# A written order for the middle of a fused spectral-filter and MLP kernel

## The chip, the cores and the metric

The kernel runs on one core of one Trainium2 chip. The metric is the device time of one execution in microseconds (us). Times inside a kernel are those of its profiled execution, counted from its first instruction.

## The reference, cut to what matters

Two residual blocks follow each other: a 2-D Fourier filter over 2048 rows of 512 values, then a squared-ReLU MLP.

```
X = rfft2(layernorm(x));  X = X * (w_r + 1j * w_i);  h = x + irfft2(X, s=(S, D)).astype(bfloat16)
r = relu(layernorm(h) @ w1 + b1);  out = h + (r * r) @ w2 + b2          # S, D, F = 2048, 512, 1792
```

The kernel computes the Fourier transforms as matmuls with tables of sines and cosines.

## The kernel before

The stretch in question takes eight "pairs" of frequency rows, 0 to 7, from the second stage of the transform to the fourth. One pair goes through these steps:

- Stage 2 on TensorE, into PSUM. ScalarE copies the result to U.
- Stage 3 on TensorE. ScalarE copies the result to X if TensorE also did the butterfly (sum and difference of two halves), or else to AB, from which VectorE makes X by two instructions.
- VectorE: two products with W (mA, mB), two combinations (the two halves of Z) and, except for pairs 0, 5 and 6, two more (the halves of M).
- Stage 4 on TensorE, from M or, where there is none, from Z. ScalarE copies the result to T; for pair 7 VectorE copies one half of it.

After pair 7 come the last stages of the transform and then the MLP, in which TensorE is busy nearly to the end. The first of them, stage 5, multiplies T by the tables GIa and GIn. The prediction and the expectations call its start the start of the MLP. VectorE's part of a pair, before the change:

```python
    ON_PE = (2, 4, 6)                     # pairs whose butterflies TensorE does
    NO_M = (5, 6)
    def spectral(pr, between=None):
        X = Xs.pop(pr)
        nxt = butterfly(pr + 1) if pr + 1 < 8 and pr + 1 not in ON_PE else (lambda: None, lambda: None)
        # [cut: tiles mA, mB; the products X * W]
        if pr > 0:
            nxt[0]()
        nc.vector.tensor_tensor(Z[:, :, 0], mA[:, :, 0], mB[:, :, 1], ALU.subtract)
        nc.vector.tensor_tensor(Z[:, :, 1], mA[:, :, 1], mB[:, :, 0], ALU.add)
        # [cut]
        nxt[1]()
        if pr > 0 and pr not in NO_M:
            # [cut: tile M]
            nc.vector.tensor_tensor(M[:, 0], Z[:, 0], Z[:, 1], ALU.add)
            nc.vector.tensor_tensor(M[:, 1], Zf[:, 3::-3], Zf[:, 1:3], ALU.subtract)
```

So where no butterfly of the next pair lies between (pairs 0, 1, 3, 5 and 7), the first half of Z stands right behind the product that it reads, and the first of M right behind its Z. With two products that follow their butterfly directly (pairs 1 and 7), that makes ten such places. The fourth stage of a pair without M reads a table of negative cosines (`en`), which VectorE makes as Cn and a DMA transposes into EI.

```python
    def cos_negs():
        nc.vector.tensor_scalar(Cn[:], EF[:, 1, 1:8, :], -1.0, None, ALU.mult)
        turned(EI[:, 1:8, 3, :], Cn[:])                    # a transposing DMA on SyncE's queue
    # [cut] in stage4, for pairs 5 and 6:
            if M is None:
                en = ei[:, 2 * P:4 * P]
                mms = [(u, r, ei[:, P:3 * P]) for u in range(2)]
                mms += [(u, 1 - r, en if u == r else ei[:, 0:2 * P]) for u in range(2)]
    # [cut] ahead of the loop over the pairs:
    cos_negs()
    for k, (dst, src) in enumerate(((W1[:], ...), (W2[:], ...), (b1b[:], ...), (b2b[:], ...))):
        load = nc.sync.dma_start(dst, src)                 # the MLP's weights and biases, same queue
```

## Time and profile before

| kernel before | |
|---|---|
| time, median of 3 runs | 164.56 us (164.55 to 164.56) |
| span in the profile | 162.8 us |
| TensorE (PE) busy | 152.1 us, 93% |
| VectorE (DVE) busy | 125.4 us, 77% |
| ScalarE (ACT) busy | 105.5 us, 65% |
| pair 7's fourth stage starts on TensorE | 45.37 us |
| stage 5's first matmuls start | 46.88 us |

The shares average over stages with different limits. In the middle, from 22 to 46 us, TensorE, VectorE and ScalarE are all nearly full. The lines are shown in the prediction.

### The profile page before, as it was taken

The numbers are of one execution on the slowest core, as the hardware profiler recorded it, in microseconds if no ns is written. First come the engines' busy times: TensorE is split into PE (matmuls) and PEld (weight loads), VectorE is DVE, ScalarE is ACT, GpSimd is POOL, SyncE is SP. The second block draws the span as 40 slices with busy tenths as digits, with TensorE's granted clock in tenths as the row PEclk, the third lists the DMA queues.
The fourth block names the chain that finished last, engine by engine and source line by source line (L and its number), as shares of the span: only waits on it lengthen the run. The fifth ranks groups of instructions, "written<-read, shape, count | busy, mean of one in ns | idle before, by whom it ended". The sixth has DMA issues, their size and how long they took to land.

```text
span 162.8 us, 2720 instructions
## 1 busy us (share of the span) xinstructions
PE 152.1 (93%) x947; PEld 87.8 (54%) x947; DVE 125.4 (77%) x320; ACT 105.5 (65%) x203; POOL 36.9 (23%) x64
## 2 busy tenths in 40 slices
PE   3999899899987999999899999999999999999990
PEld 1367675677853874666345454434454444565470
DVE  6999899999957798699995588995379984377221
ACT  4989977999978780598552797731389760288000
POOL 7868850000000005025000235000052300052000
PEclk9999999999999999999999999999999999999999
DMA  5996299998000000200000100024300005210011
GB/s 128 361 277 123 62 201 185 366 367 183 11 0 0 4 0 2 66 5 0 0 32 33 36 0 0 2 64 101 92 4 2 0 0 129 64 36 0 3 62 34
DMA packets 16430, 12.34 MB, mean 76 GB/s; under 512 B 10784, under 2 KB 14880, under 8 KB 16416
## 3 DMA queue, kind: packets, MB, share of 16 engines
q1 hardware_dynamic: 16256, 11.25, 25.1%
q0 software_dynamic: 160, 0.92, 2.5%
q8 instruction: 7, 0.11, 0.3%
q14 instruction: 7, 0.06, 0.1%
HBM read 8.01 MB, written 2.10 MB: 62 GB/s over the span
## 4 chain that ended last, share of the span: by engine, by line
PE 66%; DVE 22%; ACT 4%; issue 3%; POOL 3%; ACTq 0%; DVEq 0%; POOLq 0%
PE po L726 26%; PE ph L693 25%; DVE act L697 3%; DVE st L217 3%; PE p L346 2%; DVE mA L436 2%; PE po L714 2%; DVE mB L436 2%; PE p L590 2%; DVE Z L442 1%; POOL rs L224 1%; DVE Z L443 1%; ACT rl L696 1%; PE p L563 1%; DVE M L452 1%
## 5 line engine op out<-in xcount | busy, mean ns | idle before, releaser
L696 ACT ACTIVATE rl<-ph,b1f 128x384 bf16<-128x384 f32 (+2 forms) x70 | 41.2, 615 | 22.5 <-PE ph L693 20.7
L693 PE MATMUL ph<-UT,W 128*128 128x384 bf16 (+2 forms) x280 | 51.6, 337 | 0.6 <-DVE UT L804 0.6
L726 PE MATMUL po<-W,act 128*128 128x512 bf16 x210 | 47.6, 379 | 0.0
L697 DVE TENSOR_TENSOR act<-rl 128x384 bf16<-128x384 bf16 (+2 forms) x70 | 31.3, 483 | 9.3 <-ACT rl L696 9.1
L700 POOL TENSOR_TENSOR hb<-hs,b2b 128x512 f32<-128x512 bf16 x16 | 18.6, 1166 | 87.0 <-DVE act L697 87.0
L693 PEld LDWEIGHTS <-W 128*128 128x128 bf16 x280 | 26.9, 98 | 21.2 <-issue 1.3
L726 PEld LDWEIGHTS <-act 128*128 128x128 bf16 x210 | 20.3, 98 | 24.8 <-issue 1.7
L730 DVE TENSOR_TENSOR ot<-po,hb 128x512 bf16<-128x512 f32 x15 | 10.3, 688 | 12.6 <-PE po L726 11.1
L257 PE MATMUL p<-ones 128*128 128x512 bf16 x23 | 8.2, 511 | 2.8 <-POOL ones L153 2.8
L594 DVE SCALAR_TENSOR_TENSOR hs<-p,xs 128x512 bf16<-128x512 f32 x14 | 9.1, 681 | 0.0
L243 PE MATMUL p<-KFr,xs 128*128 128x256 bf16 x32 | 7.7, 283 | 0.8 <-DVE KFr L228 0.8
L569 ACT CAST V<-p 128x512 bf16<-128x512 f32 x14 | 8.1, 593 | 0.0
L217 DVE BATCH_NORM_STATS2 st<-xs 128x6 f32<-128x512 bf16 x12 | 7.9, 677 | 0.0
L245 PE MATMUL p<-KFr,xs 128*128 128x256 bf16 x32 | 7.6, 281 | 0.0
L257 PEld LDWEIGHTS <-ones 128*128 128x128 bf16 x32 | 3.5, 115 | 6.7 <-POOL ones L153 2.8
L346 PE MATMUL p<-GF,Bt 128*128 128x256 bf16 x56 | 7.1, 273 | 0.0
L605 ACT ACTIVATE junk<-hs 128x512 bf16<-128x512 bf16 x6 | 3.8, 628 | 5.1 <-DVE hs L594 5.1
L491 ACT CAST T<-p 128x1024 bf16<-128x1024 f32 x7 | 7.1, 1041 | 0.0
L376 ACT CAST U<-p 128x1024 bf16<-128x1024 f32 x6 | 6.2, 1059 | 0.0
L346 PEld LDWEIGHTS <-Bt 128*128 128x128 bf16 x56 | 5.4, 98 | 1.3
L620 ACT ACTIVATE sd<-mv,eps 128x1 f32<-128x1 f32 (+2 forms) x10 | 2.7, 294 | 5.1 <-DVE mv L609 5.0
L582 DVE TENSOR_TENSOR H<-V 128x254 bf16<-128x254 bf16 x14 | 6.0, 426 | 0.0
(190 smaller groups left out, 228.7 us busy)
## 6 DMA issues: line engine op xcount, KB each, us to landing
W<-in_B_w_dram SPq DMA_DIRECT2D x2, 1792.0 KB, 10.6
out_dram<-ot SPq DMA_DIRECT2D x15, 128.0 KB, 1.8
xs<-in_A_x_dram SPq DMA_DIRECT2D x3, 512.0 KB, 6.7
WB<-in_A_w_r_dram SPq DMA_DIRECT2D x1, 578.2 KB, 6.4
WB<-in_A_w_i_dram SPq DMA_DIRECT2D x1, 578.2 KB, 7.6
xs<-in_A_x_dram SPq DMA_DIRECT2D x2, 256.0 KB, 3.4
b2b<-in_B_b_dram SPq DMA_DIRECT2D x1, 128.0 KB, 9.7
out_dram<-ot SPq DMA_DIRECT2D x2, 64.0 KB, 1.5
```

Of the source, the lines that this page charges most:

```text
L217: nc.vector.bn_stats(st[:], xs[:, g, :])
L243: nc.tensor.matmul(o, lhsT=xs[:, g, P * t:P * t + P], rhs=KFr[:, g, 0:P].unsqueeze(1).to_broadcast([P, 2, P]), start=True, stop=False)
L257: nc.tensor.matmul(o, lhsT=ones[:, 0:P], rhs=ones[:], start=True, stop=True)
L346: nc.tensor.matmul(puv[:, :, e, :], lhsT=Bt[:, 2 * t + 1 - e, 2 * pr + q, :], rhs=GFv[:, t, :, e, :], start=(t == 0), stop=(t == 1))
L569: nc.scalar.copy(V[:].rearrange("p e h c -> p (e h c)"), pe[:])
L594: nc.vector.scalar_tensor_tensor(hs[:, g, :], Ys.pop(g)[:], WSC, xs[:, g, :], ALU.mult, ALU.add)
L693: nc.tensor.matmul(ph[:, 0:n], lhsT=W1[:, d, bass.ts(f, P)], rhs=UT[:, d, 0:n], start=(d == 0), stop=(d == ND - 1))
L696: nc.scalar.activation(rl[:, 0:n], ph[:, 0:n], ACT.Relu, bias=b1f[:, f:f + 1], scale=1.0)
L697: sq = nc.vector.tensor_tensor(act[:, f, 0:n], rl[:, 0:n], rl[:, 0:n], ALU.mult)
L700: add = nc.gpsimd.tensor_tensor(hb[:, g, :], hs[:, g, :], b2b[:], ALU.add)
L726: nc.tensor.matmul(po[:], lhsT=act[:, f, bass.ts(i, P)], rhs=W2[:, f, :], start=(f == 0), stop=(f == NF - 1))
L730: nc.vector.tensor_tensor(ot[:], po[:], hb[:, g, :], ALU.add)
```

## The change

Its intent: replace the loops by one written list of steps, in which halves of Z and M of neighbouring pairs alternate, so that an instruction on VectorE rarely stands right behind the one that it reads from. Along with it, TensorE does the butterflies of other pairs, and the small sine table GIn is made first on ScalarE. The diff, cut to its core:

```diff
-    ON_PE = (2, 4, 6)
+    ON_PE = (4, 6, 7)
@@ spectral() is cut into single steps: butterfly(pr, h), times_w(pr, h), to_z(pr, h), to_m(pr, h)
+    def to_z(pr, h):
+        nc.vector.tensor_tensor(Zs[pr][:, :, h], mA[:, :, h], mB[:, :, 1 - h], ALU.add if h else ALU.subtract)
@@
-    cos_negs()
     for k, (dst, src) in enumerate(((W1[:], ...), (W2[:], ...), (b1b[:], ...), (b2b[:], ...))):
@@ the loop over the pairs goes; in its place:
+    ORDER = """
+        gn.0 s3.0 s3.1 s2.2 xa.0 cn.0 xb.0 x.1 u.2 s2.3 s3.2 s2.4 A.0 B.0 b.1 c.1 y.0 A.1 B.1 z.0 y.1 u.3 x.2
+        u.4 s3.3 s2.5 s4.0 s3.4 b.2 z.1 c.2 m.1 n.1 A.2 B.2 x.3 u.5 t.0 x.4 s4.1 s2.6 s3.5 b.3 y.2 c.3 z.2 A.3
+        B.3 m.2 n.2 A.4 y.3 B.4 z.3 y.4 m.3 z.4 t.1 u.6 gi.0 x.5 s4.2 s2.7 s3.6 b.5 m.4 n.4 c.5 n.3 A.5 B.5 u.7
+        t.2 x.6 s4.4 s3.7 s4.3 A.6 y.5 z.5 B.6 y.6 z.6 t.4 x.7 t.3 sq.0 s4.5 s4.6 A.7 B.7 y.7 z.7 m.7 n.7 t.5
+        t.6 s4.7 v.7 t.7
+    """
```

A step is a name and a pair. s2, s3 and s4 are stages on TensorE; u, x and t the copies by ScalarE (xa and v by VectorE); A and B the products; b and c the butterfly; y and z the halves of Z; m and n those of M. gn and gi make the sine tables GIn and GIa, sq readies the square root, and cn is the call of cos_negs, which thereby comes behind the four loads.

More of the change, by code (lines that the diff above doesn't have):

```diff
@@ L369, in stage2_one, with copy_by, u_copy @@
         cp(Us[pr][:, q].rearrange("p (r j e) -> p r j e", r=2, e=2), o.rearrange("p (r e j) -> p r j e", r=2, e=2))
+    P2, P3, P4, Ma = {}, {}, {}, {}
+    def copy_by(dve):
+        return nc.vector.tensor_copy if dve else nc.scalar.copy
     def stage2(pr):
-        new_u(pr)
-        pu = mm_tile("p2")
+        P2[pr] = pu = mm_tile("p2")
         for q in range(2):
             stage2_half(pr, q, pu[:, 512 * q:512 * q + 512])
-        nc.scalar.copy(Us[pr][:].rearrange("p q (r j e) -> p (q r) j e", r=2, e=2),
-                       pu[:].rearrange("p (q r e j) -> p (q r) j e", q=2, r=2, e=2))
+    def u_copy(pr, dve):
+        new_u(pr)
+        copy_by(dve)(Us[pr][:].rearrange("p q (r j e) -> p (q r) j e", r=2, e=2),
+                     P2.pop(pr)[:].rearrange("p (q r e j) -> p (q r) j e", q=2, r=2, e=2))
     def stage3(pr):
@@ L381, in stage3 @@
         if pr == 0:
-            Xs[pr] = X = fwd.tile([P, 2, 2, 256], BF16, tag="X", bufs=3, name="X")
-            pxs = [mm_tile("p3"), mm_tile("p3b")]
+            P3[pr] = pxs = [mm_tile("p3"), mm_tile("p3b")]
             for u, k1 in ((0, 0), (1, 8)):
@@ L389, in stage3 @@
                 nc.tensor.matmul(o[:, 256:512], lhsT=Sn, rhs=U[:, u, 0:256], start=False, stop=True)
-            for u, cp in ((0, nc.vector.tensor_copy), (1, nc.scalar.copy)):
-                cp(X[:, u].rearrange("p r c -> p (r c)"), pxs[u][:, 0:512])
         elif pr in ON_PE:
             C, Sp, Sn, Cm = EF[:, 1, pr, :], EF[:, 0, pr, :], EF[:, 2, pr, :], Cn[:, pr - 1, :]
-            px = mm_tile("p3")
+            P3[pr] = px = mm_tile("p3")
             for u in range(2):
@@ L404, in stage3 @@
                     nc.tensor.matmul(orr, lhsT=wc, rhs=U[:, 1, other], start=False, stop=(r == 1))
-            Xs[pr] = X = fwd.tile([P, 2, 2, 256], BF16, tag="X", bufs=3, name="X")
-            nc.scalar.copy(X[:].rearrange("p u r c -> p (u r c)"), px[:])
         else:
-            px = mm_tile("p3")
+            P3[pr] = px = mm_tile("p3")
             C, Sp, Sn = EF[:, 1, pr, :], EF[:, 0, pr, :], EF[:, 2, pr, :]
@@ L413, in stage3, with new_x, x_half, x_copy @@
             nc.tensor.matmul(px[:, 512:1024], lhsT=Sp, rhs=U[:, 0, :], start=False, stop=True)
+    def new_x(pr):
+        Xs[pr] = fwd.tile([P, 2, 2, 256], BF16, tag="X", bufs=3, name="X")
+    def x_half(pr, dve):
+        u = 0 if dve else 1
+        if u == 0:
+            new_x(0)
+        copy_by(dve)(Xs[0][:, u].rearrange("p r c -> p (r c)"), P3[0][u][:, 0:512])
+    def x_copy(pr, dve):
+        px = P3.pop(pr)[:].rearrange("p (u r c) -> p u r c", u=2, r=2)
+        if pr in ON_PE:
+            new_x(pr)
+            copy_by(dve)(Xs[pr][:], px)
+        else:
@@ L414, in stage3, with butterfly @@
             ABs[pr] = AB = fwd.tile([P, 2, 2, 256], BF16, tag="AB", bufs=3, name="AB")
             for u in ((0, 1) if pr == 1 else (slice(0, 2),)):
-                nc.scalar.copy(AB[:, u], px[:].rearrange("p (u r c) -> p u r c", u=2, r=2)[:, u])
-    def butterfly(pr):
+                copy_by(dve)(AB[:, u], px[:, u])
+    def butterfly(pr, h):
         AB = ABs[pr]
-        Xs[pr] = X = fwd.tile([P, 2, 2, 256], BF16, tag="X", bufs=3, name="X")
-        bsw = AB[:, 1, ::-1, :]
-        Xf = X[:].rearrange("p u r c -> p (u r) c")
-        return (lambda: nc.vector.tensor_tensor(Xf[:, 0::3], AB[:, 0], bsw, ALU.add),
-                lambda: nc.vector.tensor_tensor(Xf[:, 2:0:-1], AB[:, 0], bsw, ALU.subtract))
@@ L428, in spectral @@
-    def spectral(pr, between=None):
-        X = Xs.pop(pr)
-        nxt = butterfly(pr + 1) if pr + 1 < 8 and pr + 1 not in ON_PE else (lambda: None, lambda: None)
-        mA = fwd.tile([P, 2, 2, 256], BF16, tag="mA", bufs=2, name="mA")
-        mB = fwd.tile([P, 2, 2, 256], BF16, tag="mB", bufs=2, name="mB")
-        step = 16 - 2 * pr if pr else 8
-        for u in ((0, 1) if pr == 0 else (slice(0, 2),)):
-            for m, w in ((mA, WB[0]), (mB, WB[1])):
-                nc.vector.tensor_tensor(m[:, u], X[:, u], w[:, pr:pr + step + 1:step, 1:Df].unsqueeze(2)
-                                        .to_broadcast([P, 2, 2, 256])[:, u], ALU.mult)
-        Zs[pr] = Z = fwd.tile([P, 2, 2, 256], BF16, tag="Z", bufs=2, name="Z")
-        ABs.pop(pr, None)
-        if pr > 0:
-            nxt[0]()
-        nc.vector.tensor_tensor(Z[:, :, 0], mA[:, :, 0], mB[:, :, 1], ALU.subtract)
-        nc.vector.tensor_tensor(Z[:, :, 1], mA[:, :, 1], mB[:, :, 0], ALU.add)
-        if between:
-            between()
-        if pr == 0:
-            nxt[0]()
-        nxt[1]()
-        if pr > 0 and pr not in NO_M:
-            Ms[pr] = M = fwd.tile([P, 2, 2, 256], BF16, tag="M", bufs=2, name="M")
-            nc.vector.tensor_tensor(M[:, 0], Z[:, 0], Z[:, 1], ALU.add)
@@ new lines, in butterfly, with times_w @@
+        if h == 0:
+            new_x(pr)
+        Xf = Xs[pr][:].rearrange("p u r c -> p (u r) c")
+        nc.vector.tensor_tensor(Xf[:, 0::3] if h == 0 else Xf[:, 2:0:-1], AB[:, 0], AB[:, 1, ::-1, :],
+                                ALU.add if h == 0 else ALU.subtract)
+    def times_w(pr, h):
+        X = Xs[pr]
+        if h == 0:
+            Ma[pr] = [fwd.tile([P, 2, 2, 256], BF16, tag=t, bufs=2, name=t) for t in ("mA", "mB")]
+        step = 16 - 2 * pr if pr else 8
+        u = slice(h, h + 1) if pr == 0 else slice(0, 2)
+        for i in (range(2) if pr == 0 else (h,)):
+            nc.vector.tensor_tensor(Ma[pr][i][:, u], X[:, u], WB[i][:, pr:pr + step + 1:step, 1:Df].unsqueeze(2)
+                                    .to_broadcast([P, 2, 2, 256])[:, u], ALU.mult)
@@ L453, in spectral, with to_m @@
+    def to_z(pr, h):
+        mA, mB = Ma[pr]
+        if h == 0:
+            Zs[pr] = fwd.tile([P, 2, 2, 256], BF16, tag="Z", bufs=2, name="Z")
+        nc.vector.tensor_tensor(Zs[pr][:, :, h], mA[:, :, h], mB[:, :, 1 - h], ALU.add if h else ALU.subtract)
+    def to_m(pr, h):
+        Z = Zs[pr]
+        if h == 0:
+            Ms[pr] = fwd.tile([P, 2, 2, 256], BF16, tag="M", bufs=2, name="M")
+            nc.vector.tensor_tensor(Ms[pr][:, 0], Z[:, 0], Z[:, 1], ALU.add)
+        else:
             Zf = Z[:].rearrange("p u r c -> p (u r) c")
-            nc.vector.tensor_tensor(M[:, 1], Zf[:, 3::-3], Zf[:, 1:3], ALU.subtract)
+            nc.vector.tensor_tensor(Ms[pr][:, 1], Zf[:, 3::-3], Zf[:, 1:3], ALU.subtract)
@@ L456, in stage4 @@
     def stage4(pr, split=False):
         Z, M = Zs.pop(pr), Ms.pop(pr, None)
-        pts = [mm_tile("p4a"), mm_tile("p4b")] if split else [mm_tile("p4")] * 2
+        P4[pr] = pts = [mm_tile("p4a"), mm_tile("p4b")] if split else [mm_tile("p4")] * 2
         ei = EI[:, pr].rearrange("p k b -> p (k b)")
@@ L484, in stage4, with t_copy @@
                 nc.tensor.matmul(o, lhsT=M[:, 1, r, e::2], rhs=ei[:, 0:2 * P], start=False, stop=True)
-        dst = T2[:, :, :, 2 * pr:2 * pr + 2, :]
-        src = [pt[:].rearrange("p (l q g s) -> p l g q s", l=4, q=2, g=G) for pt in pts]
-        if split:
-            nc.scalar.copy(dst[:, 0:2], src[0][:, 0:2])
-            nc.vector.tensor_copy(dst[:, 2:4], src[1][:, 2:4])
-        else:
-            nc.scalar.copy(dst, src[0])
+    def t_copy(pr, dve):
+        sl = slice(0, 4) if pr < 7 else slice(2, 4) if dve else slice(0, 2)
+        copy_by(dve)(T2[:, sl, :, 2 * pr:2 * pr + 2, :],
+                     P4[pr][1 if pr == 7 and dve else 0][:].rearrange("p (l q g s) -> p l g q s", l=4, q=2, g=G)[:, sl])
     new_u(0)
@@ L506, with angle_tables @@
                 after(load, ga, "the rows of W first")
-    stage3(0)
-    stage3(1)
-    stage2(2)
-    for pr in range(9):
-        if pr == 1:
-            stage3(3)
-        if pr == 3:
-            stage3(5)
-        if pr + 3 < 8:
-            stage2(pr + 3)
-        if pr == 0:
-            stage3(2)
-        if pr == 0:
+    def angle_tables(k):
+        if k == 0:
             sin_of(GIa[:], fiI[:])
-        if pr == 2:
+        else:
             nc.scalar.activation(GIn[:], fiI[:, 0:1024].bitcast(I16)[:, ::2].rearrange("p (t c) -> p t c", t=4)[:, 0::2, :],
@@ L523, with to_sqrt @@
                                  ACT.Sin, scale=-SIN_SCALE)
-        if pr in (2, 4):
-            stage3(pr + 2)
-        if pr == 4:
-            stage3(7)
-        if pr > 0:
-            stage4(pr - 1, split=(pr == 8))
-        if pr == 8:
-            warm(mm_tile("idle")[:, 0:512], 2)
-        if pr == 0:
-            spectral(0)
-        elif pr < 8:
-            spectral(pr)
-        if pr == 5:
-            nc.gpsimd.tensor_copy(b1f[:], b1b[:])
-            nc.scalar.activation(junk1[:], eps[:], ACT.Sqrt, bias=eps[:])
+    def to_sqrt():
+        nc.gpsimd.tensor_copy(b1f[:], b1b[:])
+        nc.scalar.activation(junk1[:], eps[:], ACT.Sqrt, bias=eps[:])
@@ new lines @@
+    PIECES = dict(s2=stage2, u=u_copy, s3=stage3, xa=x_half, xb=x_half, x=x_copy, b=lambda k: butterfly(k, 0),
+                  c=lambda k: butterfly(k, 1), A=lambda k: times_w(k, 0), B=lambda k: times_w(k, 1),
+                  y=lambda k: to_z(k, 0), z=lambda k: to_z(k, 1), m=lambda k: to_m(k, 0), n=lambda k: to_m(k, 1),
+                  s4=lambda k: stage4(k, split=(k == 7)), t=t_copy, v=t_copy, gi=lambda k: angle_tables(0),
+                  gn=lambda k: angle_tables(1), sq=lambda k: to_sqrt(), cn=lambda k: cos_negs())
@@ new lines @@
+    ORDER = """
[5 more added lines that the diff above has]
+    """
+    for step in ORDER.split():
+        name, k = step.split(".")
+        if name in ("u", "x", "t", "xa", "xb", "v"):
+            PIECES[name](int(k[0]), k[1:] == "v" or name in ("xa", "v"))
+        else:
+            PIECES[name](int(k))
@@ L540 @@
+    warm(mm_tile("idle")[:, 0:512], 2)
     tab.release()
```

## The prediction

> **What bounds the kernel now.** I read the page first (spans and the share of each engine), then the chain of waits in order of time, then the timelines of VectorE, ScalarE and TensorE over the stage that the change rewrites, and last the issues of the DMA queue, because the list of the changed kernel shows that one transfer changes its place there.
>
> The change touches only the stretch from 21 to 47 us: pairs 0 to 7 go from the second DFT stage to the fourth. Three engines are nearly full there. These are the busy times from the first product with W to the last combination M, and of two parts of that stretch (columns: the stretch, its length, then PE, PEld, DVE, ACT, POOL, clock, DMA share, GB/s):
>
> ```profile
> 22.70:45.60 22.90, 21.66 (x179) 16.62 (x178) 22.24 (x52) 21.34 (x25) 0.40 (x1) 1.00 0.78 213
> 28.00:38.00 10.00, 9.53 (x85) 7.43 (x83) 9.69 (x24) 10.00 (x12) 0.00 (x0) 1.00 1.00 349
> 38.00:42.60 4.60, 4.60 (x39) 3.61 (x38) 4.57 (x11) 4.36 (x5) 0.29 (x1) 1.00 0.54 67
> ```
>
> No engine has more than 1.6 us of slack in 22.9. Which one ends last is told by the chain (start, length, what):
>
> ```profile
> 40.71 0.61 DVE mB L436
> ...
> 44.09 0.42 DVE Z L442
> 44.52 0.35 DVE Z L443
> 44.89 0.43 DVE M L452
> 45.37 0.40 PE p4a L464 x2
> ```
>
> From 30 to 45 us the chain is VectorE, one instruction after another; then it passes to the eight matmuls of pair 7, to the copies of T and to the MLP, where TensorE sets the time to the end. So a microsecond won or lost where pair 7's matmuls start (45.37) reaches the end whole.
>
> Within VectorE's row what can be won is small. Its timeline (start, length) shows it at pair 3:
>
> ```profile
> 32.53 0.69 DVE L436 TENSOR_TENSOR mB<-X,WB 128x1024 bf16<-128x1024 bf16 x1
> 33.25 0.42 DVE L442 TENSOR_TENSOR Z<-mA,mB 128x512 bf16<-128x512 bf16 x1
> 33.59 0.42 DVE L443 TENSOR_TENSOR Z<-mA,mB 128x512 bf16<-128x512 bf16 x1
> 34.12 0.43 DVE L452 TENSOR_TENSOR M<-Z 128x512 bf16<-128x512 bf16 x1
> 34.46 0.42 DVE L454 TENSOR_TENSOR M<-Z 128x512 bf16<-128x512 bf16 x1
> 34.79 0.69 DVE L436 TENSOR_TENSOR mA<-X,WB 128x1024 bf16<-128x1024 bf16 x1
> ```
>
> Independent neighbours start before the record of the earlier one ends: 0.34 us after a 512-wide one (34.12 to 34.46, length 0.43), 0.61 after a 1024-wide one. An instruction that reads what its neighbour wrote waits for the whole record plus 0.03: Z starts 0.72 after mB, M starts 0.53 after Z. Such a hold costs 0.11 us, at this M 0.19.
>
> The DMA queue (start, time in the issuing sequencer):
>
> ```profile
> 25.28 1.25 SPq L260 DMA_TRANSPOSE EI<-Cn  x1
> 26.64 1.10 SPq L503 DMA_DIRECT2D W<-in_B_w_dram  x2
> 27.79 4.95 SPq L503 DMA_DIRECT2D b1b<-in_B_b_dram  x1
> 32.78 5.71 SPq L503 DMA_DIRECT2D b2b<-in_B_b_dram  x1
> ```
>
> and from issue to landing:
>
> ```profile
> W<-in_B_w_dram SPq DMA_DIRECT2D x2, 1792.0 KB, 10.6
> ...
> b2b<-in_B_b_dram SPq DMA_DIRECT2D x1, 128.0 KB, 9.7
> ...
> EI<-Cn SPq DMA_TRANSPOSE x1, 3.1
> b1b<-in_B_b_dram SPq DMA_DIRECT2D x1, 3.5 KB, 14.5
> ```
>
> The turned negative cosines (EI from Cn) land at 25.28 + 3.1 = 28.4, before 3.7 MB of weights. The engines are then full to 38 (share 1.00 in the second row above), and the two biases land at 42.3 and 42.5 (27.79 + 14.5, 32.78 + 9.7).
>
> **What the Trainium skill says.** "VectorE: DVE Perf Modes", section "The DRAIN you can't avoid", has it that a semaphore between two operations costs nothing, and adds "A next op that is not held starts earlier". The trace agrees with the second sentence only: a dependent neighbour pays 0.11 us here. "DMA: Bandwidth & Descriptors", section "Queues, rings and completion order": one issuing engine owns one ring on each of the 16 engines, and descriptors of a ring are consumed in order. The trace agrees: W's first packets move just as the last of the transposes' do, at 27.7. "Perfetto Trace Analysis", section "DMA Instruction — HWDGE (DVE, Sync)": the recorded length of an issue is descriptor generation; the data move later. The trace agrees (a 4.95 us issue of 3.5 KB lands 9.5 us after its end). "ScalarE: Activation LUTs", section "What ACT_TABLE_LOAD costs", gives about 1283 ns; the trace has 1.28 us, and the change leaves it in place.
>
> **The change part by part.**
>
> 1. Which pairs have butterflies on TensorE: 2, 4, 6 become 4, 6, 7. Three before, three after: 12 matmuls against 4 each, and VectorE keeps 8 butterfly instructions (pairs 1, 2, 3, 5 instead of 1, 3, 5, 7). The counts of all work are the same: VectorE still has 14 products of 0.61, 4 of 0.34, 16 Z, 10 M and 8 X of 0.34: 8.5 + 1.4 + 11.4 = 21.3 us. Net 0.
>
> 2. The order on VectorE. Before, the first product starts at 22.70 and the last M is done with its slot at 45.57: 22.87 us, so 1.6 us are not work. I count ten holds by a neighbour (about 1.2 us) and 0.25 us at 29.66 to 29.91 for ScalarE's copy of AB. In the written order only three neighbours remain dependent: B.6 to y.6, B.7 to y.7, z.7 to m.7: 0.36 us. The first product starts about where it did (X's copy first, then Cn: 22.74). VectorE alone would be done at 22.74 + 21.3 + 0.36 = 44.4, 1.2 earlier. I laid the whole order out with these starts (matmuls every 0.109 us for 256 columns and 0.217 for 512; ScalarE's copies every 0.90), each instruction behind its producers and buffers. The same layout of the old order ends 0.4 us early, so I use differences only: pair 7's matmuls start 0.87 us earlier than in the old layout. TensorE (pair 6's stage 4 ends 43.9) and ScalarE (last T copy back to back) are then within 0.2 us of binding too, which is why it is 0.9 and not 1.2.
>
> 3. GIn first, GIa after u.6: the 0.5 us table fits before X's second copy, where ScalarE waited 0.28 us; the 1.1 us table no longer stands ahead of pair 3's AB. It is what removes the 0.25 us above; counted already.
>
> 4. A part that the words do not name: the instruction that makes the negative cosines, with its transpose, now stands behind the loads of W1, W2, b1 and b2 in the queue. Before it was ahead. Pairs 5 and 6 are the ones without M, and their fourth stage reads this table. All four loads move up by one transpose: W1 is issued at about 25.3 (its condition, the gathers, is met near 25.1) instead of 26.64, and its data gain about 1.05 us. b2b's issue ends at 38.49 - 1.3 = 37.2, the transpose is issued then, and in ring order its packets come behind b2b's. The last packets of b2b move at 41.8 before, so 40.7 now; 896 rows of 256 bytes took about 1.1 us before; the count lands 0.3 us later. That makes 42.1 us, an estimate.
>
> 5. In the layout pair 5's fourth stage begins at 40.5 (40.9 with the drift). Two matmuls need no new table, then TensorE, in order, stands until 42.1. Behind it are 30 matmuls of 0.109 (pairs 5 and 6) = 3.3 us, then pair 7: 45.4, against 45.37 before. ScalarE's copies of pairs 5, 6 and 7 follow the matmuls as before, so nothing more is added.
>
> The sum: VectorE's order -0.9, the late table +0.9, net about 0. After the middle nothing changes.
>
> **Rivals.** (a) The table does not bind. Speaking for it: transposes without a queue ahead take 2.4 to 3.1 us to land, which from 37.2 is 40.3, and the engines are only 0.54 busy from 38 to 42.6. Then the gain is 0.9: 163.65 us. (b) The table is later than I think, since its issue may have to wait for room as b2b's 5.71 us issue seems to have done, and one ring is slow (15 of b1's 16 counts land by 41.0, the last at 42.3). A landing at 43.5 costs 1.4: 166.0. (c) ScalarE becomes the bound: it is full for ten microseconds in the second row above. The layout has it idle 0.3 and 0.7 us early on and full at the end; a slip of 0.3 would leave a gain of 0.6 if (a) holds and nothing if the table binds. (d) TensorE: the 8 further matmuls of a pair on TensorE now come late (pair 7 instead of 2) and take 0.87 us near 38 to 40, but they are in the layout and cost nothing while the table is awaited.
>
> **Range and chances.** I give (a) or near it 0.3, the table near 42.1 with 164.2 to 165.0 0.45, and (b) 0.25. The middle is 164.5 us, the range 163.6 (no wait at all) to 165.8 (landing near 43.3). 2% is 3.3 us, far outside both: faster 0.01, same 0.98, slower 0.01.
>
> **What would show it.** VectorE's holds should shrink to three and its work up to z.6 end near 41.5. TensorE should stand for 1 to 2 us before the third matmul of pair 5's fourth stage, released by a DMA (EI from Cn) and not by VectorE; the last W landing should be about 1 us earlier; pair 7's matmuls should start near 45.4. I am wrong in step 4 if that transpose lands before 41 or after 43.3, and in step 2 if VectorE stands for other waits (a copy of AB or X by ScalarE, or a Z or M buffer still read by TensorE) for more than 0.3 us in all.

## The result, and the profile after

The changed kernel took 164.37 us (median of 4 runs: 164.48, 164.49, 164.15, 164.26). The kernel before in the same rounds took 164.56. The ratio is 0.9987, with a 95% interval of 0.9970 to 1.0004: the same. Ratios here are the mean time of one kernel's runs over that of the other's of the same rounds, so not quite the ratio of the medians quoted. Executions over 1.5% slower than the fastest of the same kernel are left out of the means.

The profile explains the first of those runs (164.48). The table arrived late, as foreseen. The chain of waits of the changed kernel (start, length, what):

```profile
37.48 4.24 DMA EI<-Cn
41.72 0.04 issue
41.77 3.45 PE p L500 x30
45.22 0.02 issue
45.24 0.70 ACT T L508
...
46.17 0.58 ACT T L508
46.75 0.05 issue
46.79 0.61 PE p L770 x4
```

Before, this stretch of the chain was VectorE. Now it is a DMA from 37.48 to 41.72, then 30 matmuls of pairs 5 and 6, then ScalarE's copies to T. Stage 5 starts at 46.79, against 46.88 before.

SyncE's queue shows why the transfer starts so late (start, time in the issuing sequencer):

```profile
25.48 0.94 SPq L520 DMA_DIRECT2D W<-in_B_w_dram  x2
26.47 5.03 SPq L520 DMA_DIRECT2D b1b<-in_B_b_dram  x1
31.55 5.83 SPq L520 DMA_DIRECT2D b2b<-in_B_b_dram  x1
37.48 2.20 SPq L260 DMA_TRANSPOSE EI<-Cn  x1
```

The same transpose was issued at 25.28 before. Now it stands behind the two issues of the biases, which hold SyncE for 10.9 us (how much of this is the biases' own doing is seen in e8).

TensorE's timeline (start, length, instruction, and in brackets the idle time before it with its releaser):

```profile
40.65 0.38 PE L500 MATMUL p<-EI,Z 128*128 128x256 bf16 x2
41.77 3.44 PE L500 MATMUL p<-EI,Z 128*128 128x256 bf16 x30 [0.73 <-DMA EI<-Cn]
45.04 0.38 PE L483 MATMUL p4a<-EI,M 128*128 128x256 bf16 x2
```

Two matmuls of pair 5's fourth stage run, the third waits 0.73 us for the table, and pair 7 starts at 45.04, 0.33 us earlier than before. Of this only 0.09 reaches stage 5, because of ScalarE. Its timeline in the changed kernel, and then the one line of the kernel before that answers to the last:

```profile
43.76 0.99 ACT L508 CAST T<-p 128x1024 bf16<-128x1024 f32 x1
45.24 1.01 ACT L508 CAST T<-p 128x1024 bf16<-128x1024 f32 x1 [0.48 <-PE p L500]
46.15 0.59 ACT L508 CAST T<-p4a 128x512 bf16<-128x512 f32 x1
```

```profile
46.24 0.58 ACT L488 CAST T<-p4a 128x512 bf16<-128x512 f32 x1 [0.19 <-PE p4a L464]
```

Before, ScalarE waited 0.19 us for pair 7's matmuls. Now it waits for nothing there: it begins pair 6's copy at 45.24, when TensorE has finished that pair, and is busy with it until 46.15.

VectorE did what the new order was written for. In this timeline of the changed kernel at pairs 3 and 4, halves of Z and M of different pairs stand side by side:

```profile
33.19 0.70 DVE L456 TENSOR_TENSOR mA<-X,WB 128x1024 bf16<-128x1024 bf16 x1
33.79 0.42 DVE L463 TENSOR_TENSOR Z<-mA,mB 128x512 bf16<-128x512 bf16 x1
34.13 0.70 DVE L456 TENSOR_TENSOR mB<-X,WB 128x1024 bf16<-128x1024 bf16 x1
34.73 0.76 DVE L463 TENSOR_TENSOR Z<-mA,mB 128x512 bf16<-128x512 bf16 x2
35.41 0.43 DVE L470 TENSOR_TENSOR M<-Z 128x512 bf16<-128x512 bf16 x1
```

Every start is 0.60 us after a product or 0.34 after a half; nothing is held. And the work up to z.6 is done near 41.7. Part of that lead is lost again: with TensorE standing, the buffer that the next Z needs is not free.

```profile
43.49 0.76 DVE L463 TENSOR_TENSOR Z<-mA,mB 128x512 bf16<-128x512 bf16 x2 [0.53 <-PE p L500]
```

This wait of 0.53 us is new (about 0.1 of it is the hold by B.7, the neighbour that Z reads), and is itself a consequence of the late table.

### The profile page after: what moved, and what is told of

It is laid out like the page before. It is cut to its first block, busy times and chain, and to the rows that moved or that the text cites. A ratio compares the mean times of both kernels' runs of the same rounds, so it can differ in the third digit from the quotient of the medians.

```text
span 162.7 us, 2708 instructions
## 1 busy us (share of the span) xinstructions
PE 149.7 (92%) x934; PEld 87.5 (54%) x947; DVE 124.8 (77%) x320; ACT 105.5 (65%) x203; POOL 36.7 (23%) x64
## 4 chain that ended last, share of the span: by engine, by line
PE 62%; DVE 22%; ACT 5%; issue 3%; DMA 3%; POOL 3%; ACTq 0%; DVEq 0%; POOLq 0%
PE po L742 26%; PE ph L709 21%; DVE act L713 4%; DVE st L217 3%; DMA EI<-Cn 3%; PE p L500 2%; PE po L730 2%; ACT rl L712 2%; PE p L346 2%; PE p L606 1%; POOL rs L224 1%; DVE Z L463 1%; DVE mB L456 1%; DVE mA L456 1%; DVE hs L610 1%
## 5 line engine op out<-in xcount | busy, mean ns | idle before, releaser
L742 PE MATMUL po<-W,act 128*128 128x512 bf16 x204 | 46.8, 379 | 0.3
L257 PE MATMUL p<-ones 128*128 128x512 bf16 x22 | 7.1, 461 | 2.9 <-POOL ones L153 2.8
L243 PE MATMUL p<-KFr,xs 128*128 128x256 bf16 x32 | 7.3, 272 | 2.2 <-DVE KFr L228 2.2
L245 PE MATMUL p<-KFr,xs 128*128 128x256 bf16 x32 | 7.3, 272 | 0.0
L463 DVE TENSOR_TENSOR Z<-mA,mB 128x512 bf16<-128x512 bf16 x16 | 6.3, 422 | 0.6 <-PE p L500 0.5
```

The source lines that it names most:

```text
L257: nc.tensor.matmul(o, lhsT=ones[:, 0:P], rhs=ones[:], start=True, stop=True)
L463: nc.vector.tensor_tensor(Zs[pr][:, :, h], mA[:, :, h], mB[:, :, 1 - h], ALU.add if h else ALU.subtract)
L742: nc.tensor.matmul(po[:], lhsT=act[:, f, bass.ts(i, P)], rhs=W2[:, f, :], start=(f == 0), stop=(f == NF - 1))
```

## The experiments

The theory T: the new order is worth most of a microsecond, and the late table, which came along with it, takes most of it back. The main rivals: A, ScalarE sets the end of the middle, whatever the table does; B, the order itself is worth little. Every kernel below gave correct results. The kernel before took 164.57 us in their rounds, without one slow run of 167.95 us, and 164.52 in those of e9, which ran on another chip than e1 to e8. The changed kernel was timed in rounds of its own, in which the kernel before took 164.56.

### e1: the table ahead of the loads again

The four loads are emitted behind the step cn.0. The order of the compute engines stays as written.

```diff
-    for k, (dst, src) in enumerate((...)):   # the four loads
-        load = nc.sync.dma_start(dst, src)
+    def weights():                           # the same loop, called later
-  cn=lambda k: cos_negs()
+  cn=lambda k: (cos_negs(), weights())
```

> The changed kernel with only the order in the DMA queue changed: the four weight and bias loads are issued behind the turned negative cosines instead of ahead of them; every engine's order stays. Theory T (the new VectorE order is worth 0.9 us and the late table gives most of it back): the table lands near 28.4 us, no wait for it, pair 7's matmuls start near 44.5 (45.04 in the changed kernel), total 163.6 to 163.8 us. Rival A (ScalarE's copies of T hold the end of the middle anyway): pair 7's matmuls come earlier, but the last T copies do not; total 164.1 to 164.4. Rival B (loads 1.3 us later matter for the MLP): total 164.4 or more.

Measured: 163.89 us (163.87 to 163.92), ratio 0.9958 (0.9944 to 0.9971). TensorE no longer waits for a DMA (its timeline):

```profile
40.66 3.66 PE L500 MATMUL p<-EI,Z 128*128 128x256 bf16 x32
44.36 0.39 PE L483 MATMUL p4a<-EI,M 128*128 128x256 bf16 x2
```

Pair 7 starts at 44.36, 1.01 us earlier than before. But the time fell by 0.68 only. ScalarE's timeline shows where the rest went:

```profile
40.33 1.01 ACT L432 CAST X<-p 128x1024 bf16<-128x1024 f32 x1 [0.58 <-ACT T L508]
41.24 1.02 ACT L508 CAST T<-p 128x1024 bf16<-128x1024 f32 x1
42.28 1.28 ACT L534 ACT_TABLE_LOAD   x1
43.57 0.30 ACT L534 ACTIVATE junk<-eps 128x1 f32<-128x1 f32 x1
43.77 1.90 ACT L508 CAST T<-p 128x1024 bf16<-128x1024 f32 x2
45.57 0.60 ACT L508 CAST T<-p4a 128x512 bf16<-128x512 f32 x1
```

From 40.33 to the last copy nothing waits. That copy starts 0.67 us earlier than before (46.24), not 1.01. The time lies between the two forecasts, 0.09 above T's range and 0.21 below A's. So T holds in the main: the changed kernel with the table early wins 0.68 us (its choice of pairs included, see e3), and the late table costs 164.37 - 163.89 = 0.48, give or take the spread of the changed kernel's runs (164.15 to 164.49). And A is partly right: ScalarE swallows 0.34 of what TensorE wins.

### e2: the late table in the old order

```diff
-    cos_negs()
     for k, (dst, src) in enumerate((...)):   # the four loads
         [cut]
+    cos_negs()
```

> The kernel before with only the negative cosines' transpose moved behind the four loads. Theory T: the table lands near 41.7 as in the changed kernel, but in the old order pair 5's fourth stage asks for it at 41.5, and TensorE has 0.43 us to spare before pair 7; so 0 to 0.15 us slower, 164.55 to 164.7. If a late table costs by itself what it took from the changed kernel (0.7 us), 165.2.

Measured: 164.57 us (164.55 to 164.81), ratio 1.0003 (0.9990 to 1.0017). The transpose landed at 41.70, as late as in the changed kernel. TensorE's timeline:

```profile
41.31 3.87 PE L481 MATMUL p<-EI,Z 128*128 128x256 bf16 x32
45.39 0.39 PE L464 MATMUL p4a<-EI,M 128*128 128x256 bf16 x2 [0.21 <-DVE M L452]
```

In the old order pair 5 begins 0.66 us later, so the table is hardly missed: the 32 matmuls take 3.87 us where they take 3.66 without a wait. TensorE has that time to spare, because it must wait for VectorE's first M of pair 7 in any case: 0.43 us in the kernel before, 0.21 here. So the late table costs something only where the order is fast enough to need it.

### e3: the choice of pairs alone

```diff
-    ON_PE = (2, 4, 6)      # in the kernel before
+    ON_PE = (4, 6, 7)
```

> The kernel before with only the choice of pairs changed: butterflies on TensorE for 4, 6, 7 in place of 2, 4, 6. Theory T: same counts, about one or two holds fewer on VectorE and pair 7's further matmuls on TensorE near 39 us, so 164.3 to 164.6 (-0.1 by the layout). A rival in which the choice of pairs, not the order, makes the gain on VectorE: 163.7 to 163.9.

Measured: 164.49 us (164.46 to 164.51), ratio 0.9994 (0.9981 to 1.0007). Pair 7 starts at 45.29 instead of 45.37. The choice of pairs is worth 0.08 us in the old order, no more.

### e4: the table later still

A load of 448 KB that nothing needs stands between W2 and the biases, ahead of the transpose.

```diff
                                     (W2[:], B_w2.rearrange("(i p) d -> p i d", p=P)),
+                                    (extra[:], B_w1[0:P]),
```

> The changed kernel with one further load of 448 KB between W2 and the biases (to a tile that nobody reads), so that the table comes later still. Theory T: at 365 GB/s it takes 1.25 us; the table lands near 43.0 and every bit of that reaches the end: total 165.5 to 165.8. Rival A (ScalarE holds the end): less than half of it, 164.4 to 165.0.

Measured: 168.12 us (166.83 to 168.69), ratio 1.0213 (1.0182 to 1.0245), which leaves it unclear whether it is 2% slower. I expected too small a delay: the profiled run is the fastest of them (166.83), and in it the transpose landed at 44.08, 2.36 us later than in the changed kernel. Its TensorE timeline:

```profile
44.13 3.44 PE L501 MATMUL p<-EI,Z 128*128 128x256 bf16 x30 [3.07 <-DMA EI<-Cn]
47.40 0.38 PE L484 MATMUL p4a<-EI,M 128*128 128x256 bf16 x2
```

The wait is 3.07 us instead of 0.73. Pair 7 starts 2.36 us later, and the span grows by 2.4, from 162.7 to 165.1. So between these two profiled executions each microsecond of the landing was a microsecond of the kernel. The size of the delay was my error; the slope is what the run was for. The other five runs took up to 168.69, and no profile tells where their table landed.

### e5: dependent neighbours again, table early

e1, with the written order permuted on VectorE so that halves follow the instruction that they read: 17 dependent neighbours instead of 3. The other engines' lists stay.

```diff
-  A.0 B.0 b.1 c.1 y.0 A.1 B.1 z.0 y.1 ... b.2 z.1 c.2 m.1 n.1 A.2 B.2 ... b.3 y.2 c.3 z.2 A.3 B.3 m.2 n.2
+  A.0 B.0 y.0 z.0 b.1 c.1 A.1 B.1 y.1 ... z.1 m.1 n.1 b.2 c.2 A.2 B.2 ... y.2 z.2 m.2 n.2 b.3 c.3 A.3 B.3
```

> Table first (as the first experiment), and on VectorE the same instructions put back so that each reads what its neighbour wrote: 17 or so holds instead of 3, the counts unchanged. Theory T (holds are what the new order saves, 0.11 us each): 14 holds more are 1.5 us of VectorE, 1.6 us later at the start of the MLP by the layout; total 165.2 to 165.6. Rival: the order of holds is worth little because ScalarE or TensorE bind as well; total 163.9 to 164.4.

Measured: 165.30 us (165.28 to 165.33), ratio 1.0043 (1.0028 to 1.0058), 1.41 us above e1. Part of VectorE's timeline:

```profile
33.35 0.69 DVE L456 TENSOR_TENSOR mB<-X,WB 128x1024 bf16<-128x1024 bf16 x1
34.14 0.76 DVE L463 TENSOR_TENSOR Z<-mA,mB 128x512 bf16<-128x512 bf16 x2
35.00 0.42 DVE L470 TENSOR_TENSOR M<-Z 128x512 bf16<-128x512 bf16 x1
```

Z starts 0.79 us after mB and M 0.86 after the pair of Z, where steps of the same kinds in the changed kernel, shown above, took 0.60 and 0.68. These two holds are among the longer ones (0.19 and 0.18). The last M of pair 7 starts at 45.88 here and at 44.22 in e1: 1.66 us for 14 holds, 0.12 each on average. This refutes B, since the instructions are the same and only their order differs. It is not the old order, which had ten such places: the seven that the change removed are worth about 0.8 us at this price (an estimate), of the 1.01 by which VectorE's last M comes earlier in e1 than before (45.23 to 44.22).

### e6: the sine tables at their old places

e1, with gi.0 moved to just before x.3 and gn.0 to just before x.4.

```diff
-  gn.0 s3.0 s3.1 ...  A.2 B.2 x.3 u.5 t.0 x.4 ...  t.1 u.6 gi.0 x.5
+  s3.0 s3.1 ...  A.2 B.2 gi.0 x.3 u.5 t.0 gn.0 x.4 ...  t.1 u.6 x.5
```

> Table first, and the two angle tables back where they were on ScalarE: GIa ahead of pair 3's copy of AB, GIn ahead of pair 4's X. Theory T: VectorE's buffer of AB hides it now, the layout shows no change; 163.85 to 164.1. Rival (GIn first is what makes the gain): 164.2 or more.

Measured: 163.88 us (163.85 to 163.90), ratio 0.9956 (0.9941 to 0.9971), as e1. "GIn first" is worth nothing in the new order.

### e7: the last copies shared

If ScalarE swallows 0.34 us, giving VectorE half of pair 6's copy should win some of it back. In e1, pair 6's fourth stage goes into two PSUM tiles and the copy into two halves.

```diff
-  pts = [mm_tile("p4a"), mm_tile("p4b")] if split else [mm_tile("p4")] * 2
+  pts = [mm_tile("p4a"), mm_tile("p4b")] if pr >= 6 else [mm_tile("p4")] * 2
-            pt = pts[0]
+            pt = pts[e]
-  t.5 t.6 s4.7 v.7 t.7         # plus the slices of t_copy
+  t.5 t.6 v.6 s4.7 v.7 t.7
```

> Table first, and pair 6's copy of T shared like pair 7's: the fourth stage of pair 6 writes two PSUM tiles, ScalarE copies one half and VectorE, which is idle then, the other. In the first experiment ScalarE is full from 40.3 us to the last copy (45.57) while pair 7's first half is complete near 45.2. Theory (ScalarE's copies are the bound of the end of the middle once the table is early): last copy 0.35 us earlier, total 163.5 to 163.65. Rival (VectorE and TensorE bind): 163.85 to 163.95.

Measured: 163.74 us (163.73 to 163.75), ratio 0.9948 (0.9934 to 0.9963). This is the fastest kernel, but it won 0.15 us where I expected 0.24 or more and the rival forecast 0.04 or less. Its chain of waits shows what took over:

```profile
43.86 0.91 ACT T L508
44.77 0.04 issue
44.81 0.38 PE p4b L483 x2
45.19 0.22 PE p4a L483 x2
45.41 0.22 PE p4b L483 x2
45.62 0.43 PE idle L257 x2
46.05 0.03 issue
46.08 0.72 PE p L771 x4
```

Pair 7's second tile (p4b) has to wait for ScalarE's copy of pair 5 to free a PSUM tile (44.77), so TensorE starts it at 44.81. Stage 5 starts at 46.08; in e1 it started at 46.22.

### e8: the table between the weights and the biases

The changed kernel, with only the two bias loads moved behind cn.0.

```diff
-     (W2[:], ...), (b1b[:], ...), (b2b[:], ...))):
+     (W2[:], ...))):
+ def biases():  # the two loads
-  cn=lambda k: cos_negs()
+  cn=lambda k: (cos_negs(), biases())
```

> The changed kernel with only the two bias loads moved behind the negative cosines' transpose; it still comes behind W1 and W2. Theory T: its packets follow W2's, which land near 38.5, so it lands near 39.5, one microsecond before pair 5's third matmul asks for it (40.9): no wait, 163.85 to 164.0 as with the table first. If 3.7 MB of weights ahead are already too many: 164.2 to 164.5.

Measured: 163.85 us (163.85 to 163.86), ratio 0.9955 (0.9940 to 0.9970): all of e1's gain, and no wait for a DMA. Of SyncE's queue (start, time in the sequencer), and the table's time from issue to landing:

```profile
25.34 0.95 SPq L518 DMA_DIRECT2D W<-in_B_w_dram  x2
26.38 8.28 SPq L260 DMA_TRANSPOSE EI<-Cn  x1
34.70 0.59 SPq L523 DMA_DIRECT2D b1b<-in_B_b_dram  x1
35.35 4.40 SPq L524 DMA_DIRECT2D b2b<-in_B_b_dram  x1
```

```profile
EI<-Cn SPq DMA_TRANSPOSE x1, 14.4
```

Behind the weights alone the transpose is in time, but only just. It landed near 40.75 (26.38 + 14.4), not at 39.5 as I expected, and the third matmul of pair 5, the first that reads the table, starts at about 40.88 (40.66 and two matmuls of 0.109). So standing behind the weights put off the landing by some 12 us, from 28.3 in the kernel before, and that used up nearly all the slack. Standing behind the biases as well added the last microsecond, to 41.72, and that one binds. Nor are the 10.9 us of the biases' issues all their own: here, behind the transpose, they take 0.59 and 4.40, and it is the transpose, next behind the weights, whose issue takes 8.28.

### e9: shared copies with the table late

e7's split of pair 6's copy, in the changed kernel with its late table.

> The changed kernel as it is (table late), with only pair 6's copy of T shared between ScalarE and VectorE. In the changed kernel pair 7's matmuls start 0.33 us earlier than before but the last copies only 0.09 and 0.35 earlier, because ScalarE's copy of pair 6 starts at 45.24 and ends at 46.15. If that copy is what swallows the rest: last ScalarE copy near 45.85 instead of 46.15, total 0.15 to 0.25 lower than the changed kernel's, 164.1 to 164.25. If it does not matter: 164.3 to 164.5.

Measured: 164.27 us (164.04 to 164.81), ratio 0.9994 (0.9980 to 1.0008). In the profiled runs, the table landed at the same moment (41.71, and 41.72 in the changed kernel), ScalarE's last copy started at 45.88 instead of 46.15, and the span fell from 162.7 to 162.4. ScalarE's line shows that the wait has gone back to TensorE:

```profile
45.88 0.59 ACT L508 CAST T<-p4a 128x512 bf16<-128x512 f32 x1 [0.61 <-PE p4a L483]
```

So ScalarE's copy of pair 6 did cost the changed kernel about 0.25 us. The medians differ by 0.10 only (0.06 when each is taken against the kernel before of its own rounds), and the runs of both kernels spread more than that, so the timed runs alone are inconclusive.

## Why the prediction was right or wrong, point by point

The time, 164.37, lies within the range and 0.13 under the middle, and "the same" was right. The mechanism, a gain by order given back to a late table, is confirmed from both sides: without the late table the kernel is faster (e1, e8), with a later one slower by as much as it is later (e4, in the profiled run). The sum was "-0.9, +0.9". It measured -0.68 and +0.48. Both terms were too large and their errors partly cancel, so that the total came so near the middle is in part luck.

- **Step 1, the choice of pairs, "Net 0".** About right: -0.08 us by itself (e3).
- **Step 2, VectorE's order, -0.9.** Where it was computed, at pair 7's matmuls, it was slightly low: 0.87 predicted, 1.01 measured (e1). At the end it was too high, since 0.34 of it is lost to ScalarE. The price of a hold, 0.11, is confirmed (0.12 in e5), and three holds were left, as counted. VectorE alone was to be done at 44.4; in e1 it is at 44.56 (the last M's start at 44.22 and a slot of 0.34). The 11.4 us in that sum are 34 slots of 0.335, which is nearer the trace than the 0.34 written beside it.
- **Step 3, GIn first.** The step credited the new place of the tables with removing a wait of 0.25 us. In the new order this is worth 0.01 at most (e6). VectorE does not wait for pair 3's AB there either, so the new place of the tables was not needed to remove that wait.
- **Step 4, the late table.** The transpose was predicted to be issued at 37.2 and to land at 42.1; it was issued at 37.48 and landed at 41.72. The loads moved up by 1.16 us (W1's issue from 26.64 to 25.48), but the second of the weights landed 2.3 us earlier (at 38.5; 40.8 before), not about 1. TensorE stood for 0.73 us and not "for 1 to 2", since the landing was 0.38 earlier.
- **Step 5, "nothing more is added".** This is the term that was mis-sized. Pair 7's matmuls started at 45.04, not 45.4. But ScalarE's copy of pair 6 lasts until 46.15, and 0.24 of TensorE's 0.33 us ended there. The same limit makes the late table a little cheaper: against e1 it delays TensorE by 45.04 - 44.36 = 0.68 us, but ScalarE's last copy only by 46.15 - 45.57 = 0.58 (the two profiled runs differ by 0.61, the medians by 0.48).

Of the rivals, (a) would have been 163.65; with the table early the kernel takes 163.89, so even its full size was 0.24 too large, for ScalarE's sake. (b) did not happen; e4 shows what it would have cost. (c), ScalarE as the bound, was half of the truth, and I had given it a slip of 0.3. (d) is not seen: without the late table TensorE runs pairs 5 and 6 with no wait.

The last part of the prediction said that step 2 would be wrong if VectorE stood for other waits of more than 0.3 us. By the letter it was: VectorE stood 0.53 us for a Z buffer. In e1, with the table early, VectorE's last M starts at 44.22, against 44.63 in the changed kernel, so this wait belongs to step 4.

Two things stay open. In e1, and within 0.03 us in the other kernels with the written order, ScalarE starts its copy of pair 7's X at 40.33, though TensorE's matmuls for it end at 39.95. In e5, whose order on VectorE differs, it is 41.75 after 41.37. The profile names nothing that explains the 0.38 us between them. This is at the head of ScalarE's full stretch, so it may be worth as much at the end. And the kernels with a late table vary from run to run (164.15 to 164.49; e9 164.04 to 164.81; e4 166.83 to 168.69), while e1, e6, e7 and e8 stay within 0.05 us. I take it that the landing varies, but only profiled executions show a landing, so that is argued and not shown.

## What to carry to other kernels

When a list of steps is rewritten, look at what else moves with it: here one call slipped behind four loads in a DMA queue, and cost 0.48 of the 0.68 us that the new order had won. Behind two of them it was in time, with little more than 0.1 us to spare (e8), so look at the landing and not only at whether something waits. Between dependent instructions on VectorE put independent ones of a neighbouring tile; the instructions stay the same, and here it won about 0.1 us per place (e5). Where three engines are nearly full, compute a gain to the start of the next stage and through every engine that feeds it, since the next one to become full (here ScalarE's copies) takes its part.

## What the Trainium skill lacked or had wrong

- "VectorE: DVE Perf Modes", section "The DRAIN you can't avoid", reports eight copies in a row that took as long with a semaphore after each as with one after the last, and says that it costs nothing extra there. That does not carry over to this kernel: a dependent neighbour starts 0.11 us later than an independent one, at some places 0.19, and 14 such places cost 1.41 us of the kernel's time (e5 against e1, the same instructions in another order). The page's remark that an operation which is not held starts earlier agrees with this; it gives no size.
- "Perfetto Trace Analysis", section "DMA Instruction — HWDGE (DVE, Sync)", lists what the recorded issue spans, but not how much it grows with what stands ahead in the queue. The same transpose was recorded with 1.25 us (before, ahead of the loads), 2.20 us (changed kernel, behind all four) and 8.28 us (e8, right behind the weights), and landed 3.1, 4.2 and 14.4 us after its issue. The next issue of SyncE began only after it. So a small transfer behind large ones landed late here and held up the issues behind it.
- No page that I read has the run-to-run spread of a landing that the kernel waits for. The changed kernel's times spread over 0.34 us, those with the table early over 0.05 (e1). That the landing is what varies is not shown.
